# Attention block on one core: the score matmuls of a VectorE row are released together and picked by free heads, and the order is laid out anew

## The chip, the core and the metric

One core of a Trainium2 chip runs the whole kernel. The metric is the time of one launch in device microseconds; lower is better. The engines named here are TensorE (PE; its weight loads are PEld), ScalarE (ACT), VectorE (DVE), GpSimd (POOL) and the DMA queue of SyncE (SP).

## The reference

Self-attention over 2048 tokens, 16 heads of 28, all data in bf16:

```python
B, S, D = x.shape            # 1, 2048, 448
qkv = (x @ wqkv).reshape(B, S, 3, 16, 28).transpose(2, 0, 3, 1, 4)
scores = einsum("bhqd,bhkd->bhqk", q, k) * 28 ** -0.5
p = softmax(scores, axis=-1)
o = einsum("bhqk,bhkd->bhqd", p, v)
return o.transpose(0, 2, 1, 3).reshape(B, S, D) @ wo
```

## The kernel before

**Tiling.** The heads form 4 groups of 4, the queries 4 chunks of 512. A pair of group and chunk is a *unit* (16 of them, 0 to 15). A unit has 16 *rows*, one for each 128 keys, and a row has 4 *tiles*, one a head: 128 keys by 512 queries. That makes 256 rows and 1024 tiles. The head h of a group lies on the partitions 32h to 32h+27 of QT and KT, so a tile's score matmul uses one quarter of TensorE's rows, and matmuls of different heads can stand in the array together.

**Two ways for exp.** 189 rows take the exponential on ScalarE: their 756 tiles are taken in turn in groups of three and two; one *score group* S0, S1, ... is one matmul a tile into three banks of PSUM (0 to 2) or two (3 and 4), and one activation E0, E1, ... (L950) turns the group into PT. So even groups are three-wide, odd ones two-wide, 303 in all, and group i+2 needs the banks that E*i* has read. The other 67 rows (PLAN["rows"]) go to VectorE: each of their tiles has a score matmul of its own (SD*row*_*head*, here a *ride*) into one bank of the pool M (banks 5 to 7), VectorE turns it into integers whose bits are an exponential (D1, L912, into DY), and when the row has all four, two more passes over the row (DS, L920) make shifted copies.

**Behind the scores.** A PV pass is four matmuls, one a head, side by side in TensorE's columns: one pass for a ScalarE row (PT with V), three for a VectorE row (DY with V, DS with VW), all added up in one bank of M for a unit. When a unit is done, VectorE copies the bank to OTS, and the row sums are inverted and spread over the partitions: by DMAs through DRAM for most units, by small fp32 matmuls for unit 14 (N1, L748, and N2, L759) and unit 15. After the last group's units come the output projections (OP, L700). The projections of x to q, k and v (L545, four passes a job; L562, four steps a job) also go through the banks of M, spread over the first 11 units by the due times in PLAN["late"].

**What sets the order.** Every operation is an entry with an engine, its dependencies, a guessed duration and a priority. schedule() plays the engines forward in time: on each it takes, of the entries that could start within a look-ahead of the earliest one (CFG["plook"], 477 ns, on TensorE), the one of least priority. A ride's priority carries CFG["sdpen"] if the entry before it on TensorE is no score matmul. The guessed durations come from pe_dur(): a step within a kind 220 ns, a switch between score matmuls (kind "r") and passes (kind "c") 100 more, a score matmul behind one without a common head 60. Where TensorE would do too little in a window, fill_to() puts in zero passes (L474) or pads a score group with zero matmuls (L891). Each engine then runs its list strictly in that order and waits by semaphores, so the guesses set the order, not the time.

The score group and its activation:

```python
s = P.add("pe", (lambda e, ...: s_mm(e, tl, range(bf(), bf() + 3), DH, s_op[0].pad)), deps=deps, after=[last_s[0]],
          kind="r", units=1.0, act=112.0 * len(tl), heads=tuple(h for _, _, h in tl), ..., name=f"S{gi}", ...)
ex = P.add("act", (lambda e, ...: e.activation(PT[:, p0 * 512:(p0 + w) * 512], bank(bf(), w), AF.Exp, scale=ESCALE)),
           deps=[s] + ..., after=[last_exp[0]], dur=66 + w * 426.67, prio=pr, name=f"E{gi}", ...)
```

A ride (in row_tile): it may not stand ahead of its partner, the group that it was released with.

```python
s = P.add("pe", (lambda e, ...: s_mm(e, [t], [hold[0].banks[0]], DH)), deps=deps, after=[partner, old],
          kind="r", units=1.0, act=112.0, heads=(h,), prio=p_pr + 0.0001, name=f"SD{r}_{h}", acq=("M", 1), acq_slack=ASLACK)
s.ride = True
```

Of the kernel before, what the change touches and what calls it, by code (L numbers as in the profile page):

```python
# [63 lines left out]
class _Prog:  # L64
# [49 lines left out]
    def pe_dur(self, prev, op, t):  # L114

        if op.kind is None:
            return op.dur
        one, switch = (430.0 if t < self.COLD else 220.0), 100.0
        if prev is None or prev.kind != op.kind:
            return switch + one * op.units  # L120
        if op.kind == "r" and op.heads and not set(op.heads) & set(prev.heads):
            return 60.0
        return one * op.units

    def schedule(self):
        ops = self.ops
# [16 lines left out]
        order = {e: [] for e in ENGINES}  # L143
        nsched = 0
        pools = self.pools
        acc_open = [None]
        recent = []

        def fill_to(st, nxt):

# [39 lines left out]
        while nsched < n:  # L190
            best = None
            for e in ENGINES:
                if not avail[e]:
                    continue
                ft = free_t[e]
                sts = [(start_of(i, ft), i) for i in avail[e]]
                sts = [(a, i) for a, i in sts if a is not None]
                if not sts:
                    continue
                mn = min(a for a, i in sts)  # L200
                look = CFG["dlook"] if e == "dve" else CFG["plook"] if e == "pe" else self.BIGLOOK
                cand = [(a, i) for a, i in sts if a <= mn + look]
                off = CFG["sdpen"] if e == "pe" and not (order[e] and order[e][-1].kind == "r") else 0.0
                st, i = min(cand, key=lambda t: (ops[t[1]].prio + (off if ops[t[1]].ride else 0.0), t[1]))
                if st > mn + min(self.LOOKAHEAD, look):
                    fit = [(a, k) for a, k in sts if a <= mn + min(self.LOOKAHEAD, look) and a + ops[k].dur <= st]
                    if fit:
                        st, i = min(fit, key=lambda t: (ops[t[1]].prio, t[1]))
                if best is None or (st, ops[i].prio, i) < best[0]:
                    best = ((st, ops[i].prio, i), e, i)  # L210
# [125 lines left out]
ZLO = -ZADD  # L336


CFG = {"late": 4.5, "load": 1.5, "load0": 18, "dcost": 2.3, "dlead": 31.565328345, "aslack": 232.311784294, "opp": 0.0, "oload": 2.5, "klead": 0.388752986, "vlag": 0.115386484, "hot1": 45000.0, "hotm": 3600.0, "nslack": 2278.659670856, "dlook": 20.0, "plook": 477.119826734, "rcost": 4.9, "rlead": 1.0, "rend": 4, "rgap": 2, "acost": 0.4455, "dprio": 0.137295812, "nride": 2, "rslack": 300.0, "stail": 24, "jprio": -2.367501222, "vwlead": 0.517534586, "sdpen": 6.828329237, "rcostx": -0.000676632}

PLAN = {
    "rows": [9, 14, 19, 21, 26, 32, 36, 37, 43, 48, 51, 54, 57, 58, 61, 67, 74, 78, 83, 85, 90, 95, 96, 99, 103, 104, 107, 111, 113, 118, 119, 126, 128, 133, 136, 142, 143, 145, 147, 155, 160, 164, 170, 171, 175, 176, 180, 181, 187, 190, 192, 194, 197, 199, 207, 208, 211, 215, 216, 219, 221, 228, 229, 232, 239, 242, 243],
    "late": [1.299322759, 1.822557006, 2.163875537, 1.596356936, 2.063296816, 1.856206612, 1.946155059, 2.196917245, 2.351631723, 2.650591028, 2.763613996, 3.528403009, 3.047534614, 3.721148513, 4.223385591, 3.69651624, 3.88002907, 4.051839957, 4.449835317, 4.560752685, 5.643247141, 5.99397256, 6.330386924, 6.513825751, 5.809406098, 6.003720398, 6.187280726, 6.225029866, 8.237463635, 8.012219161, 7.61108487, 7.334748232, 7.574370741, 6.838411391, 7.65064537, 7.734259839, 8.315962664, 7.954788714],
}


def _fast(nc, x, wqkv, wo, out, n_heads=16):
# [35 lines left out]
    with es:  # L383
# [543 lines left out]
        for gi, (kind, idx, b0) in enumerate(items):  # L927
# [14 lines left out]
            else:  # L942
# [5 lines left out]
            s_op.append(s)  # L948
            last_s[0] = s
            ex = P.add("act", (lambda e, p0=p0, w=w, bf=bf: e.activation(PT[:, p0 * 512:(p0 + w) * 512], bank(bf(), w), AF.Exp, scale=ESCALE)),  # L950
                       deps=[s] + [slot_last.get(("A", p0 + j)) for j in range(w)], after=[last_exp[0]], dur=66 + w * 426.67, prio=pr, name=f"E{gi}",
                       rel=[(s, 0)] if b0 is None else [])
            last_exp[0] = ex
            ex.relpool = [("T", b) for b, k_ in t_free.items() if k_ == gi]
# [779 lines left out]
```

## Time and profile before

| | before |
|---|---|
| median of 3 runs | 363.78 us (363.62 to 364.08) |
| the profiled execution | 364.01 us, span 362.2 us |
| granted TensorE clock | 1.00 |
| PE busy | 350.9 us (97%), 3894 matmuls |
| ACT busy | 345.9 us (95%), 303 of 307 instructions are exps |
| DVE busy | 321.4 us (89%), 574 instructions |
| HBM read, written | 7.23 MB, 2.06 MB |

Busy times are of the span. TensorE's matmuls are pipelined and their ends are modelled; ScalarE's recorded durations overlap, an exp's record beginning before that of the last one ends. What an exp or a matmul costs is therefore read from the start of one to the start of the next.

### The profile page before, as it was taken

To read this page: it belongs to the slowest core of one execution; us is meant where nothing else is said; L and a number is where in the kernel's file an instruction comes from. 1 tells how busy PE (TensorE), PEld (TensorE's weight loads), DVE (VectorE), ACT (ScalarE), POOL (GpSimd) and SP (SyncE) were. 2 spreads that over 40 slices of the span, in tenths; PEclk is the share of its full clock that TensorE was granted. 3 is DMA by queue.
4 is the path that set the end of the run, shared out by engine and by line. 5 is a ranking of instruction groups with operands and counts; after the bars stand their busy time and mean duration, and the time that the engine had idled before them with its cause. 6 is when DMAs were issued, how large, how long until landed. Compare 5 with 4: busy or idle time off the path is not lost.

```text
span 362.2 us, 8855 instructions
## 1 busy us (share of the span) xinstructions
PE 350.9 (97%) x3894; PEld 118.1 (33%) x3894; DVE 321.4 (89%) x574; ACT 345.9 (95%) x307; POOL 3.4 (1%) x9
## 2 busy tenths in 40 slices
PE   8999999999999999999999999999999999999996
PEld 4443233233333323232233343322222222223423
DVE  6678978888998899999999999899999999999624
ACT  1999999999999999999999999999999999999892
POOL 3000000000000000000000000000000000000000
PEclk9999999999999999999999999999999999999999
DMA  8500000000000000010000100000000000010111
GB/s 238 144 2 3 4 30 3 21 14 4 30 2 5 32 5 31 2 32 2 3 32 6 33 3 31 2 5 30 4 31 11 23 4 32 2 62 22 53 53 53
DMA packets 12549, 9.93 MB, mean 27 GB/s; under 512 B 4768, under 2 KB 10656, under 8 KB 12504
## 3 DMA queue, kind: packets, MB, share of 16 engines
q1 hardware_dynamic: 11704, 8.63, 8.1%
q8 instruction: 32, 0.52, 0.6%
q10 hardware_dynamic: 800, 0.66, 0.5%
q14 instruction: 13, 0.11, 0.1%
HBM read 7.23 MB, written 2.06 MB: 26 GB/s over the span
## 4 chain that ended last, share of the span: by engine, by line
ACT 73%; PE 23%; DVE 3%; issue 0%
ACT PT L950 73%; PE ps L888 8%; PE ps L855 7%; PE ps L474 2%; PE ps L700 2%; PE ps L545 2%; DVE DY L912 2%; PE ps L562 1%; PE ps L528 1%; PE ps L779 1%; DVE DS L920 0%; PE ps L759 0%; PE ps L822 0%; PE ps L798 0%; PE ps L748 0%
## 5 line engine op out<-in xcount | busy, mean ns | idle before, releaser
L950 ACT ACTIVATE PT<-ps 128x1536 bf16<-128x1536 f32 (+1 forms) x303 | 342.9, 1356 | 1.9 <-PE ps L888 1.1
L912 DVE TENSOR_SCALAR DY<-ps 128x512 int16<-128x512 f32 x268 | 174.6, 682 | 10.7 <-PE ps L888 10.0
L888 PE MATMUL ps<-QT,KT 28*128 28x512 bf16 x1024 | 164.1, 383 | 6.2 <-ACT PT L950 2.7
L920 DVE TENSOR_SCALAR DS<-DY 128x2048 int16<-128x2048 int16 x134 | 90.0, 680 | 0.6
L888 PEld LDWEIGHTS ps<-QT,KT 28*128 28x128 bf16 x1024 | 42.2, 91 | 127.4 <-ACT PT L950 84.4
L855 PE MATMUL ps<-PT,V 128*32 128x512 bf16 x756 | 66.0, 386 | 0.5 <-DVE OTS L713 0.2
L855 PE MATMUL ps<-DS,VW 128*32 128x512 f16 x536 | 47.4, 384 | 0.2 <-DVE DS L920 0.2
L545 PE MATMUL ps<-xT,w_raw 112*32 112x512 bf16 x512 | 36.1, 382 | 0.0
L474 PE MATMUL ps<-ZM,ZW 128*32 128x512 bf16 x316 | 28.6, 410 | 1.2 <-DVE ZM L456 1.2
L855 PEld LDWEIGHTS ps<-PT,V 128*32 128x32 bf16 x756 | 16.7, 94 | 34.7 <-issue 28.7
L855 PE MATMUL ps<-DY,V 128*32 128x512 f16 x268 | 26.4, 385 | 0.2
L855 PEld LDWEIGHTS ps<-DS,VW 128*32 128x32 bf16 x536 | 12.7, 94 | 18.3 <-issue 12.8
L545 PEld LDWEIGHTS ps<-xT,w_raw 112*32 112x32 bf16 x512 | 12.7, 96 | 15.0 <-issue 4.2
L562 PE MATMUL ps<-w_raw,xT 112*128 112x112 bf16 x256 | 17.1, 214 | 0.0
L688 DVE CAST OUTS<-ps 128x448 bf16<-128x448 f32 x14 | 8.7, 620 | 8.2 <-PE ps L700 7.4
L562 PEld LDWEIGHTS ps<-w_raw,xT 112*128 112x128 bf16 x256 | 13.0, 98 | 7.1 <-issue 4.2
L518 DVE CAST KT<-ps 128x512 bf16<-128x512 f32 x16 | 11.0, 686 | 4.6 <-PE ps L545 4.6
L474 PEld LDWEIGHTS ps<-ZM,ZW 128*32 128x32 bf16 x316 | 7.7, 99 | 15.2 <-issue 11.4
L518 DVE CAST V<-ps 128x448 bf16<-128x448 f32 x16 | 9.9, 619 | 3.1 <-PE ps L562 3.1
L700 PE MATMUL ps<-wop,XO 128*128 128x448 bf16 x48 | 11.7, 356 | 0.0
L516 DVE TENSOR_SCALAR QT<-ps 128x512 bf16<-128x512 f32 x15 | 10.3, 687 | 1.1 <-PE ps L545 1.1
L855 PEld LDWEIGHTS ps<-DY,V 128*32 128x32 bf16 x268 | 7.0, 94 | 11.4 <-issue 7.7
(51 smaller groups left out, 85.6 us busy)
## 6 DMA issues: line engine op xcount, KB each, us to landing
RB<-scr_r SPq DMA_DIRECT2D x14, 256.0 KB
out_dram<-OUTS SPq DMA_DIRECT2D x14, 112.0 KB, 1.7
XO<-in_x_dram SPq DMA_DIRECT2D x3, 448.0 KB, 8.0
w_raw<-in_wqkv_dram SPq DMA_DIRECT2D x2, 392.0 KB, 7.4
wop<-in_wo_dram SPq DMA_DIRECT2D x16, 24.5 KB
XO<-in_x_dram SPq DMA_DIRECT2D x1, 224.0 KB, 3.7
XO<-in_x_dram ACTq DMA_DIRECT2D x1, 224.0 KB, 4.0
scr_l<-OTS SPq DMA_DIRECT2D x14, 8.0 KB
```

The lines of the kernel that those rows point to most:

```text
L474: ins = e.matmul(ps[32 * h:32 * h + 32, b * 512:(b + 1) * 512], ZW[:, :], ZM[:, :], start=shut, stop=shut, skip_group_check=not shut, tile ...
L516: fe = (lambda e: e.tensor_scalar(evac[0](), evac[1](hold[0].banks[0]), mul, None, ALU.mult))
L518: fe = (lambda e: e.tensor_copy(evac[0](), evac[1](hold[0].banks[0])))
L545: ins = e.matmul(ps[32 * h:32 * h + 32, b * 512:(b + 1) * 512], w_raw[0:IT, it, col:col + 32], xT[0:IT, it, c * 512:(c + 1) * 512], start= ...
L562: ins = e.matmul(ps[:, b * 512 + j * GD:b * 512 + (j + 1) * GD], xT[0:IT, it, n * 128:(n + 1) * 128], w_raw[0:IT, it, 2 * D + g * GD:2 * D ...
L688: fe = (lambda e: e.tensor_copy(OUTS[:, oi, :], bank(hold.banks[0])[:, 0:D]))
L700: return e.matmul(bank(hold[0].banks[0])[:, 0:D], OTN[:, gg, n * 128:(n + 1) * 128], wop[:, gg, :], start=(gg == 0), stop=(gg == G - 1))
L855: ins = e.matmul(ps[32 * h:32 * h + 32, b * 512:(b + 1) * 512], weights(k, h), p_[h], start=(kt == 0 and k == 0), stop=(kt == NK - 1 and k ...
L888: ins = e.matmul(bank(b), KT[32 * h:32 * h + rows, g, kt * 128:(kt + 1) * 128], QT[32 * h:32 * h + rows, g, c * QCH:(c + 1) * QCH], start= ...
L912: o1 = P.add("dve", (lambda e, ri=ri, h=h, s=s: e.tensor_scalar(DY[:, ri, h * 512:(h + 1) * 512], bank(s.banks[0]), ZLO, ZADD, ALU.max, AL ...
L920: row_ev[r] = [P.add("dve", (lambda e, k=k: e.tensor_scalar(DS[:, k, rk, :], DY[:, ri, :], float(PHASE[k + 1]), None, ALU.add)), deps=row_ ...
L950: ex = P.add("act", (lambda e, p0=p0, w=w, bf=bf: e.activation(PT[:, p0 * 512:(p0 + w) * 512], bank(bf(), w), AF.Exp, scale=ESCALE)), deps ...
```

## The change

1. *Release.* Before, a score group released at most two rides, of heads that it doesn't hold itself and that the row still lacked (nride 2). Now the first group that comes near enough to a row (dlead) releases the row's four rides at once.
2. *Choice.* schedule() keeps run_heads, the heads of the score matmuls that stand directly behind each other at the end of TensorE's list; another kind of entry, or a head that comes a second time, empties it. A ride's priority now carries sdpen if the run is empty, sdlap if it shares a head with the run, and nothing if it doesn't. pe_dur() compares with the run too, not with the last entry alone.
3. *Guess.* The planner's duration of an exp is 51 + w * 426.67 ns instead of 66 + w * 426.67.
4. *Layout.* PLAN["rows"] (67 rows as before, others), PLAN["late"] and ten of CFG's other weights have new values.

```diff
-        if op.kind == "r" and op.heads and not set(op.heads) & set(prev.heads):
+        if op.kind == "r" and op.heads and not set(op.heads) & self.run_heads:
             return 60.0
...
+        run_heads = self.run_heads = set()
...
-                off = CFG["sdpen"] if e == "pe" and not (order[e] and order[e][-1].kind == "r") else 0.0
-                st, i = min(cand, key=lambda t: (ops[t[1]].prio + (off if ops[t[1]].ride else 0.0), t[1]))
+                run = run_heads if e == "pe" else None
+                st, i = min(cand, key=lambda t: (ops[t[1]].prio + (0.0 if not ops[t[1]].ride else CFG["sdpen"] if not run else CFG["sdlap"] if set(ops[t[1]].heads) & run else 0.0), t[1]))
...
                 recent.append((op.t1, op.act))
+                if op.kind != "r" or (run_heads & set(op.heads)):
+                    run_heads.clear()
+                if op.kind == "r":
+                    run_heads.update(op.heads)
...
-CFG = {..., "dlead": 31.565328345, ..., "dprio": 0.137295812, "nride": 2, ..., "sdpen": 6.828329237, ...}
+CFG = {..., "dlead": 28.484612267, ..., "dprio": 0.366065749, "nride": 4, ..., "sdlap": 2.562717941, ..., "sdpen": 5.516852626, ...}
 PLAN = {
-    "rows": [9, 14, 19, 21, 26, 32, 36, 37, 43, ...],
+    "rows": [8, 14, 21, 23, 24, 28, 36, 40, 41, ...],
...
-                       ..., dur=66 + w * 426.67, prio=pr, name=f"E{gi}",
+                       ..., dur=51 + w * 426.67, prio=pr, name=f"E{gi}",
...
-                for h in free[:CFG["nride"]]:
+                for h in (free[:int(CFG["nride"])] if CFG["nride"] < 4 else (3, 2, 1, 0)):
                     have.append(h)
                     row_tile(r, h, s, pr - 5)
```

The file grows by five lines ahead of the kernel's body: L888 becomes L893, L545 L550, L562 L567, L855 L860, L700 L705, L748 L753, L759 L764, L474 L479, L912 L917, L920 L925 and L950 L955.

Two places on TensorE. First the window behind a two-wide score group into which a projection's four passes were put, near a third of the run. Before, score group 96 (heads 0, 1, 2), a ride of head 1 (the row that waits for f_dve), group 97 (two-wide), two PV passes, the projection, group 98:

```order
L888 MATMUL ps<-QT,KT 128x512 [waits f_act]
L888 MATMUL ps<-QT,KT 128x512 x2
L888 MATMUL ps<-QT,KT 128x512 [waits f_dve]
L888 MATMUL ps<-QT,KT 128x512 [waits f_act]
L888 MATMUL ps<-QT,KT 128x512
L855 MATMUL ps<-PT,V 32x512 x8
L545 MATMUL ps<-xT,w_raw 32x512 [waits f_dve]
L545 MATMUL ps<-xT,w_raw 32x512 x15
L888 MATMUL ps<-QT,KT 128x512 [waits f_act]
```

Now, at such a place: group 81 (two-wide, heads 3 and 0), a ride of head 2, one PV pass, a projection, group 82:

```order
L893 MATMUL ps<-QT,KT 128x512 [waits f_act]
L893 MATMUL ps<-QT,KT 128x512
L893 MATMUL ps<-QT,KT 128x512 [waits f_dve]
L860 MATMUL ps<-PT,V 32x512 x4
L550 MATMUL ps<-xT,w_raw 32x512 [waits f_dve]
L550 MATMUL ps<-xT,w_raw 32x512 x15
L893 MATMUL ps<-QT,KT 128x512 [waits f_act]
```

The ride has moved from behind a group that shares its head to behind one that doesn't, and one PV pass has left the window.

Second the normalisation of unit 14 in the tail. Before, its second half (L759, three quarters and then the last one behind three zero passes) stands behind group 288, which is three-wide, after an output projection:

```order
L888 MATMUL ps<-QT,KT 128x512 [waits f_act]
L888 MATMUL ps<-QT,KT 128x512 x2
L700 MATMUL ps<-wop,XO 128x448 [waits f_dve]
L700 MATMUL ps<-wop,XO 128x448 x3
L759 MATMUL ps<-id_f,RS 32x128 [waits f_dve]
L759 MATMUL ps<-id_f,RS 32x128 x11
L474 MATMUL ps<-ZM,ZW 32x512 x12
L759 MATMUL ps<-id_f,RS 32x128 x4
```

Now it stands behind group 287, which is two-wide and directly follows group 286:

```order
L893 MATMUL ps<-QT,KT 128x512 [waits f_act]
L893 MATMUL ps<-QT,KT 128x512 x2
L893 MATMUL ps<-QT,KT 128x512 [waits f_act]
L893 MATMUL ps<-QT,KT 128x512
L479 MATMUL ps<-ZM,ZW 32x512 x8
L705 MATMUL ps<-wop,XO 128x448 [waits f_dve]
L705 MATMUL ps<-wop,XO 128x448 x3
L764 MATMUL ps<-id_f,RS 32x128 [waits f_dve]
L764 MATMUL ps<-id_f,RS 32x128 x15
```

The zero passes have moved ahead of the output projection and are two instead of three, and the whole second half stands in one piece, one group earlier.

More of the change, by code (lines that the diff above doesn't have):

```diff
@@ L336 @@
 ZLO = -ZADD
-CFG = {"late": 4.5, "load": 1.5, "load0": 18, "dcost": 2.3, "dlead": 31.565328345, "aslack": 232.311784294, "opp": 0.0, "oload": 2.5, "klead": 0.388752986, "vlag": 0.115386484, "hot1": 45000.0, "hotm": 3600.0, "nslack": 2278.659670856, "dlook": 20.0, "plook": 477.119826734, "rcost": 4.9, "rlead": 1.0, "rend": 4, "rgap": 2, "acost": 0.4455, "dprio": 0.137295812, "nride": 2, "rslack": 300.0, "stail": 24, "jprio": -2.367501222, "vwlead": 0.517534586, "sdpen": 6.828329237, "rcostx": -0.000676632}
+CFG = {"late": 4.5, "load": 1.5, "load0": 18, "dcost": 2.3, "dlead": 28.484612267, "aslack": 234.39592858, "opp": 0.0, "oload": 2.5, "klead": 0.4323975, "vlag": 0.111436825, "hot1": 45000.0, "hotm": 3600.0, "nslack": 2491.286802307, "dlook": 20.0, "plook": 475.978771878, "rcost": 4.9, "rlead": 1.0, "rend": 4, "rgap": 2, "acost": 0.4455, "dprio": 0.366065749, "nride": 4, "rslack": 300.0, "stail": 24, "jprio": -1.39984025, "sdlap": 2.562717941, "vwlead": 0.511450916, "sdpen": 5.516852626, "rcostx": -0.000676632}
@@ L341 @@
 PLAN = {
-    "rows": [9, 14, 19, 21, 26, 32, 36, 37, 43, 48, 51, 54, 57, 58, 61, 67, 74, 78, 83, 85, 90, 95, 96, 99, 103, 104, 107, 111, 113, 118, 119, 126, 128, 133, 136, 142, 143, 145, 147, 155, 160, 164, 170, 171, 175, 176, 180, 181, 187, 190, 192, 194, 197, 199, 207, 208, 211, 215, 216, 219, 221, 228, 229, 232, 239, 242, 243],
-    "late": [1.299322759, 1.822557006, 2.163875537, 1.596356936, 2.063296816, 1.856206612, 1.946155059, 2.196917245, 2.351631723, 2.650591028, 2.763613996, 3.528403009, 3.047534614, 3.721148513, 4.223385591, 3.69651624, 3.88002907, 4.051839957, 4.449835317, 4.560752685, 5.643247141, 5.99397256, 6.330386924, 6.513825751, 5.809406098, 6.003720398, 6.187280726, 6.225029866, 8.237463635, 8.012219161, 7.61108487, 7.334748232, 7.574370741, 6.838411391, 7.65064537, 7.734259839, 8.315962664, 7.954788714],
+    "rows": [8, 14, 21, 23, 24, 28, 36, 40, 41, 49, 50, 52, 53, 56, 63, 69, 70, 75, 81, 84, 92, 95, 96, 99, 103, 107, 109, 111, 114, 118, 120, 126, 133, 134, 135, 140, 141, 145, 150, 151, 161, 164, 165, 172, 174, 176, 177, 181, 184, 187, 190, 191, 193, 198, 200, 209, 210, 212, 218, 220, 222, 229, 232, 234, 236, 242, 243],
@@ new lines @@
+    "late": [0.985671578, 1.7329246, 2.288014113, 1.339252415, 3.3302101, 1.724823683, 1.811463685, 2.191018136, 2.31384295, 2.705035917, 3.075950617, 3.785215586, 3.262105589, 3.600600612, 4.037198031, 4.358459457, 3.422715306, 4.857595707, 4.052828262, 4.565812919, 5.085450579, 6.945699915, 6.701297875, 7.57212228, 5.328799148, 5.744658604, 6.006846096, 6.663843099, 7.985857407, 10.303312002, 7.510487333, 7.372796781, 7.921217652, 7.444661772, 7.671904113, 8.161370786, 7.99358382, 8.734219075],
@@ L950, in _fast @@
             ex = P.add("act", (lambda e, p0=p0, w=w, bf=bf: e.activation(PT[:, p0 * 512:(p0 + w) * 512], bank(bf(), w), AF.Exp, scale=ESCALE)),
-                       deps=[s] + [slot_last.get(("A", p0 + j)) for j in range(w)], after=[last_exp[0]], dur=66 + w * 426.67, prio=pr, name=f"E{gi}",
+                       deps=[s] + [slot_last.get(("A", p0 + j)) for j in range(w)], after=[last_exp[0]], dur=51 + w * 426.67, prio=pr, name=f"E{gi}",
                        rel=[(s, 0)] if b0 is None else [])
```

## The prediction

> **What bounds the kernel now.** I read the page first: busy times, the chain that ended last, the costliest groups.
>
> ```profile
> PE 350.9 (97%) x3894; PEld 118.1 (33%) x3894; DVE 321.4 (89%) x574; ACT 345.9 (95%) x307; POOL 3.4 (1%) x9
> ACT 73%; PE 23%; DVE 3%; issue 0%
> L950 ACT ACTIVATE PT<-ps 128x1536 bf16<-128x1536 f32 (+1 forms) x303 | 342.9, 1356 | 1.9 <-PE ps L888 1.1
> ```
>
> ScalarE is busy nearly from end to end with 303 exps (L950). By the group's row only 1.9 us of idle time stand before them, which would leave a new order nothing to win. But recorded exps overlap, so that idle time hides lateness, and I read the starts instead, from the timeline of ScalarE (start, duration; each row is from a window so narrow that it holds few exps): the first exp, two undisturbed ones, three pairs of which the second is late, and the last exp.
>
> ```profile
> 10.28 1.45 ACT L950 ACTIVATE PT<-ps 128x1536 bf16<-128x1536 f32 x1 [0.71 <-PE ps L891]
> ...
> 46.35 1.53 ACT L950 ACTIVATE PT<-ps 128x1536 bf16<-128x1536 f32 x1
> 47.68 1.12 ACT L950 ACTIVATE PT<-ps 128x1024 bf16<-128x1024 f32 x1
> ...
> 67.81 1.34 ACT L950 ACTIVATE PT<-ps 128x1024 bf16<-128x1024 f32 x1
> ...
> 99.70 1.08 ACT L950 ACTIVATE PT<-ps 128x1024 bf16<-128x1024 f32 x1
> 100.96 1.45 ACT L950 ACTIVATE PT<-ps 128x1536 bf16<-128x1536 f32 x1 [0.18 <-PE ps L888]
> ...
> 120.36 1.12 ACT L950 ACTIVATE PT<-ps 128x1024 bf16<-128x1024 f32 x1
> 121.44 1.45 ACT L950 ACTIVATE PT<-ps 128x1536 bf16<-128x1536 f32 x1
> ...
> 222.72 1.09 ACT L950 ACTIVATE PT<-ps 128x1024 bf16<-128x1024 f32 x1
> 223.81 1.45 ACT L950 ACTIVATE PT<-ps 128x1536 bf16<-128x1536 f32 x1
> ...
> 353.69 0.74 ACT L950 ACTIVATE PT<-ps 128x512 bf16<-128x512 f32 x1
> ```
>
> A three-wide exp holds ScalarE for 47.68 - 46.35 = 1.33 us. Between 47.68 and 67.81 lie nine undisturbed pairs: 20.13 / 9 = 2.237 us a pair, so a two-wide one takes 0.90. The 151 pairs from 10.28 to 353.69 would need 337.7 us and take 343.4: **5.7 us are lost** to late starts. The exp at 100.96 is late by 1.26 - 0.90 = 0.36 us, though its row names 0.18. That loss is what the change can touch; everything else is 151 pairs, a start and a tail.
>
> Why exps start late shows on TensorE. Here it works up to the exp at 121.44 (PEld row: weight load of score group 97; PE rows: its matmuls are not a row of their own, the merged row before them is left out):
>
> ```profile
> 119.27 0.09 PEld L888 LDWEIGHTS ps<-QT,KT 28*128 28x128 bf16 x2 [0.60 <-ACT PT L950]
> ...
> 119.59 0.61 PE L855 MATMUL ps<-PT,V 128*32 128x512 bf16 x8
> 120.03 1.04 PE L545 MATMUL ps<-xT,w_raw 112*32 112x512 bf16 x16
> 121.00 0.39 PE L888 MATMUL ps<-QT,KT 28*128 28x512 bf16 x4
> 121.33 0.40 PE L855 MATMUL ps<-PT,V 128*32 128x512 bf16 x4
> 121.55 0.39 PE L855 MATMUL ps<-DY,V 128*32 128x512 f16 x4
> 121.87 0.39 PE L888 MATMUL ps<-QT,KT 28*128 28x512 bf16 x3
> 122.19 0.62 PE L855 MATMUL ps<-DS,VW 128*32 128x512 f16 x8
> 122.74 0.60 PE L888 MATMUL ps<-QT,KT 28*128 28x512 bf16 x4
> ```
>
> The two-wide group 97 gets its banks at 119.27, which is 0.24 after the exp before its own began (120.36 - 1.33). Then come two PV passes, four projection passes and, at 121.00, the three-wide group 98; its exp begins 0.44 later and 0.18 late. So between a two-wide group and the next three-wide one TensorE has 1.33 + 0.90 - 0.44 - 0.24 = **1.55 us**; this window took 1.73. Between a three-wide group and a two-wide one there is some 0.4 us more to spare, and overruns can be carried.
>
> Step prices from the same rows: pass to pass 0.22 (121.33 to 121.55); pass to scores 0.32 (121.55 to 121.87); scores to pass 0.32 (121.87 to 122.19). A VectorE score tile (a "ride") next to a group that leaves its head free adds nothing: group 98 with its ride has x4 in 0.39, as three matmuls have. With a common head it adds a pass: x4 in 0.60 at 122.74.
>
> **The change: work on TensorE.** I counted both orders step by step. Neighbouring score tiles with a common head: 160 before, 64 now; of the rides directly behind a group, 88 shared a head and now 2 do. That is 96 x 0.21 = 20.2 us less. But score work is entered and left more often, 304 times against 284: 20 x (0.32 + 0.32 - 0.22) = 8.4 us more. Net TensorE needs about 11.8 us less.
>
> The Trainium skill ("TensorE: Matmul & The Clock Gate", Back-to-back issue gap) gives 131 ns for a 512-column matmul in a sustained stream; by that the 96 conflicts would be worth only 12.6 us and the net 4.2. The row of 0.60 against 0.39 disagrees with it here, and I go by the row.
>
> The Trainium skill ("TensorEngine Tiling (Array Packing)", Key Properties) also speaks against the new order: changing the tiling mode drains the array, a price that the 20 new visits pay. The trace agrees (0.32 instead of 0.22 a switch), and the 8.4 us hold it.
>
> TensorE's saved time is no saved time of the kernel: most of it only lengthens waits for ScalarE. It counts where a window ran over. So I split the 5.7 us.
>
> (1) Over-full windows. By these prices ten two-wide windows before the tail need over 1.55 us (behind groups 79, 81, 87, 97, 163, 165, 173, 175, 179, 187: mostly five or six passes), together 2.1 us over. Eight of the exps behind them are late, by 1.67 us together, from 100.96 (0.36) through 121.44 (0.18) to 223.81 (1.09 - 0.90 = 0.19). In the new order there are five (137, 157, 195, 197, 267), together 0.83 over; in the same proportion 0.66 late. Gain 1.0. Windows such as the one behind the new group 81 (ride, PV, four projections: 0.01 + 0.31 + 4 x 0.216 + 0.32 = 1.50) now fit.
>
> (2) Four late exps behind full windows in a row (128, 130, 192, 274), 0.5 us; the same tally gives two now (104, 136), 0.35. Gain 0.15.
>
> (3) The remaining late starts before the tail: 5.7 - 1.3 (the tail, below) - 1.67 - 0.5 = 2.2 us, some 18 of 0.03 to 0.17 us and many smaller. Their windows fit by the prices, and most hold a ride, so I put them to rides that wait for VectorE to empty a bank, and to steps a little over price. A row of the waits (us, times, longest), two of the groups and one of the windows (stretch, length, busy us and counts by engine, granted clock, DMA):
>
> ```profile
> PEld ps L888 <- DVE DY L912: 20.3, 60, 0.5
> L891 PE MATMUL ps<-ZM 28*128 28x512 bf16 x17 | 2.3, 374 | 0.0
> L474 PE MATMUL ps<-ZM,ZW 128*32 128x512 bf16 x316 | 28.6, 410 | 1.2 <-DVE ZM L456 1.2
> 60.00:330.00 270.00, 264.45 (x2938) 83.12 (x2935) 258.95 (x454) 269.73 (x240) 0.00 (x0) 1.00 0.06 17
> ```
>
> Rides wait for VectorE 60 times, 0.34 us each. The bounds of this term: all 2.2 us stay, or they shrink like the rest of the tally (2.5 us of overrun before the tail becomes 1.1, carried lateness included), a gain of 1.2. More slack behind a ride helps, the wait itself stays: I take 0.5, nearer to the first. In it are the padding matmuls (L891), 3 instead of 17, inside score groups.
>
> (4) The tail, where unit 14's normalisation stands between score groups (ScalarE, then TensorE):
>
> ```profile
> 334.45 1.58 ACT L950 ACTIVATE PT<-ps 128x1536 bf16<-128x1536 f32 x1
> 336.26 2.37 ACT L950 ACTIVATE PT<-ps 128x1024 bf16<-128x1024 f32 x2 [0.23 <-PE ps L888]
> 337.18 1.44 ACT L950 ACTIVATE PT<-ps 128x1536 bf16<-128x1536 f32 x1
> 339.36 1.02 ACT L950 ACTIVATE PT<-ps 128x1024 bf16<-128x1024 f32 x1 [0.74 <-PE ps L888]
> ...
> 334.18 0.93 PE L700 MATMUL ps<-wop,XO 128*128 128x448 bf16 x4
> 334.95 0.95 PE L748 MATMUL ps<-SEL,OTS 128*128 128x4 f32 x8
> ...
> 336.41 0.93 PE L700 MATMUL ps<-wop,XO 128*128 128x448 bf16 x4
> 337.27 0.86 PE L759 MATMUL ps<-id_f,RS 128*32 128x128 f32 x24
> 337.95 0.83 PE L474 MATMUL ps<-ZM,ZW 128*32 128x512 bf16 x12
> 338.60 0.40 PE L759 MATMUL ps<-id_f,RS 128*32 128x128 f32 x8
> ```
>
> Exps 287 and 289 are late by 1.81 - 1.33 = 0.48 and 2.18 - 1.33 = 0.85, 1.33 us together. The change takes one output projection from behind group 286 and a zero pass (337.95, three before, two now), but puts each half of the normalisation behind a two-wide group, where there is less room. Added up from these rows, the new windows behind 285, 287 and 289 run over by 0.4, 0.9 and 0.4; the same addition gives 1.9 for before where 1.33 was measured, so 1.2 is left. Gain 0.15, between -0.4 and 0.5.
>
> Free or equal: exp, VectorE and DMA instructions are the same in kind and number; TensorE's order is the same up to score group 2 and behind the last group, so start (10.28) and tail after 353.69 stay. The zero passes stay 316 matmuls. The planner's exp price (66 to 51 ns) only orders.
>
> Sum: 1.0 + 0.15 + 0.5 + 0.15 = **1.8 us** less. The profiled execution took 364.01 (span 362.2), so 362.2; the median of the runs is 0.23 lower, 363.78 - 1.8 = **362.0 us**. From the terms' bounds (1.0 within 0.6 to 1.2) this case lies between 360.8 and 363.0. About 0.2%, 0.73 us, is what a measurement of this kernel can tell from no change.
>
> **Rivals.**
>
> *Slower: rides block TensorE's queue.* All four tiles of a row stand ready now, and 149 of them directly behind a group whose head they don't touch (54 before). Each still waits for VectorE to empty one of three banks, with PV passes and the next group behind it. In the new order 40 two-wide windows hold a ride and have under 0.34 us to spare; a wait of 0.34 in each would run over by 6.9 us. VectorE is busy 89% of the span and its 60 waits speak for it; that TensorE already waits for it before, for a share of 2.2 us only, against. It decides from about 2.5 of the 6.9 us; with half of them, 362.0 + 3.4 = 365.4. Chance 0.09. The Trainium skill ("TensorE: Matmul & The Clock Gate", Part 3) says that matmuls start and end strictly in order, which is this mechanism; the chance rests on the rows.
>
> *Slower: the granted clock.* Less work on TensorE could let its clock drop; it was 1.00 throughout 60 to 330 us. A pass would double to 0.43: a stretch of three exps (3.4 us) with some 2.6 us of steps would need 5.2, about 1.8 us late; three such stretches give 367. The unchanged zero passes speak against it. Chance 0.03.
>
> *No change.* The late starts are VectorE's more than TensorE's conflicts, term (3) stays whole, the tail loses its 0.4, and the new over-full windows cost their full 0.83: gain 0.4, 363.4. Chance 0.14.
>
> *Much faster.* Terms (1) to (3) vanish altogether: 363.78 - 4.4 = 359.4. Chance 0.06. That the change doesn't do what it says is out: the order shows 2 conflicts behind groups where 88 stood.
>
> **How the numbers follow.** The forecast has 0.68. Its upper end (363.0 to 363.05) still counts as faster, so faster has 0.68 + 0.06 = 0.74, no change 0.14, slower 0.12. The range: below 360.8 lies most of the much faster case, above 363.7 the slower ones and a little of no change, together under 0.2.
>
> **What would show it.** In the profile after: late starts from first to last exp of about 3.9 us instead of 5.7; rides within 0.39 us of their group; waits of L888's weight loads for ScalarE above 84 us; start and end of the exp stream apart by about 341.6. Wrong: waits for VectorE far above 20.3 us with late exps behind rides; a clock below 1.00; late exps in the tail above 1.8 us.

## The result and the profile after

The changed kernel took 366.5 us (median of 9 runs, 364.85 to 373.66), the kernel before 363.78 (9 runs, 363.62 to 364.16). The ratio is 1.0048 [1.0031, 1.0065]; it leaves out the longest runs, 372 to 374 us, in which TensorE's clock was at half speed for about 20 us. The forecast of 362.0 us was wrong in sign.

The profiled execution was one of those long ones (373.66 us, span 371.5). The same kernel was profiled once more at full clock (after_again below): 365.24 us, span 363.1. Both are needed. First the page of the long one: its span, busy times, ScalarE's slices, the granted clock in tenths over 40 slices, the chain, and the exps' group (busy, mean ns, idle).

```profile
span 371.5 us, 8829 instructions
PE 353.1 (95%) x3880; PEld 115.1 (31%) x3880; DVE 324.8 (87%) x574; ACT 346.8 (93%) x307; POOL 3.4 (1%) x9
ACT  1999999999999999999999766999999999999892
PEclk9999999999999999999999655999999999999999
ACT 73%; PE 21%; DMA 2%; DVE 2%; issue 1%; SPq 0%
L955 ACT ACTIVATE PT<-ps 128x1536 bf16<-128x1536 f32 (+1 forms) x303 | 343.8, 1388 | 10.5 <-PE ps L893 9.4
```

Before, every digit of PEclk was 9 and 1.9 us of idle time stood before the exps:

```profile
PEclk9999999999999999999999999999999999999999
```

Now 10.5 us of idle time do, three slices show a clock of 0.5 to 0.6, and ScalarE starves in the same three. The damage has a place, 204 to 232 us. The timeline there, TensorE with its weight loads, and one row of ScalarE:

```profile
204.91 0.10 PEld L860 LDWEIGHTS ps<-PT,V 128*32 128x32 bf16 x4 [0.23 <-issue]
204.92 0.40 PE L860 MATMUL ps<-PT,V 128*32 128x512 bf16 x4
...
205.34 0.39 PE L893 MATMUL ps<-QT,KT 28*128 28x512 bf16 x2
...
207.20 0.40 PE L860 MATMUL ps<-PT,V 128*32 128x512 bf16 x4 [1.48 <-issue]
...
208.21 0.62 PE L860 MATMUL ps<-DS,VW 128*32 128x512 f16 x4
...
209.41 2.37 ACT L955 ACTIVATE PT<-ps 128x1536 bf16<-128x1536 f32 x2 [1.87 <-PE ps L893]
```

At 205.72 TensorE stops for 1.48 us with "issue" as the reason: it waits for nothing that the profile shows. Behind the stop, passes of 0.40 us become passes of 0.62. The exp at 209.41 (E174) starts 2.13 us late, where before's E174 was 0.20 late. The next view cuts the profile into stretches (length; busy us and counts by engine; granted clock; DMA), with the cuts put where the trace's clock record changes:

```profile
201.03:204.44 3.41, 3.41 (x52) 1.64 (x50) 2.69 (x7) 3.41 (x4) 0.00 (x0) 1.00 0.07 26
204.45:207.86 3.41, 1.91 (x23) 0.51 (x19) 2.44 (x5) 3.09 (x3) 0.00 (x0) 1.00 0.02 5
207.87:231.75 23.88, 23.88 (x159) 4.44 (x158) 15.86 (x26) 16.00 (x14) 0.00 (x0) 0.50 0.03 9
231.76:235.17 3.41, 3.41 (x37) 0.93 (x33) 2.99 (x6) 3.41 (x4) 0.00 (x0) 1.00 0.07 26
```

A stretch of 3.41 us holding the stop (TensorE busy for 1.91 of it) is followed by 23.88 us at exactly half clock, seven times 3.41. In the profile at full clock the same stop, 1.20 us, falls otherwise into the stretches, and the clock stays:

```profile
206.86 0.40 PE L860 MATMUL ps<-PT,V 128*32 128x512 bf16 x4 [1.20 <-issue]
...
203.56:206.97 3.41, 2.19 (x34) 0.73 (x30) 3.26 (x7) 3.41 (x4) 0.00 (x0) 1.00 0.02 5
206.98:210.39 3.41, 3.16 (x36) 0.85 (x28) 2.55 (x5) 2.39 (x3) 0.00 (x0) 1.00 0.02 5
```

Late starts from E0 to E302, counted as the prediction does but with 50.6 + 426.67 ns a tile as an exp's price (1.331 us three-wide, 0.904 two-wide; the rows gave 1.33 and 0.90): 6.00 us before, 15.39 in the long profile, 7.03 in the one at full clock.

**What stops TensorE.** The trace records a taken branch of TensorE there, from 205.33 to 207.14. The program holds a second, general path for inputs that the fast one does not cover, and it lies in the middle of each engine's code. The fast path jumps over it at a named operation; a hint at another named operation announces the jump (PV8_8 is the PV pass of unit 8 and row 8; a third number, as in PV8_8_1, counts the passes of a VectorE row from the second one on):

```python
P.HINT_AT = {"pe": "PV8_8", "dve": f"NM{NU - 2}", "act": exps[-6]}
P.JUMP_AT = {"pe": "PV8_11", "dve": f"OPEV{n0 - 1}", "act": f"OPEV{n0}", "sp": "L1_0"}
```

The diff does not touch these lines, but it moves what stands between the two names. From hint to jump it was 5.12 us before (196.28 to 201.40); in the new order it is 3.17 us (202.16 to 205.33). One 16 KB packet on queue 8 follows the hint; by its time it brings the target's code. The DMA view of 204.7 to 205.9 us in the long profile holds just that packet (packets, MB, share):

```profile
q8 instruction: 1, 0.02, 5.0%
```

It ran from 204.80 to 205.76, when TensorE had been at the jump since 205.33; the jump ended 1.39 us after the landing. Before, it ran from 197.83 to 198.81, long ahead of the jump, which took 0.33 us. The Trainium skill ("Runtime: NRT & Kernel Launch", Instruction fetch mechanics) says that instructions are prefetched in sequence only, in blocks of 16 KiB, and that a taken branch to a page that isn't there waits for its DMA. The stop agrees; in the kernel before, where a packet came behind the hint and ahead of the jump, the jump had nothing to wait for.

### The profile page after: what moved, and what is told of

Read it like the earlier page. It is cut to its first block, busy times and chain, and to the rows that moved or that the text cites. A ratio compares the mean times of both kernels' runs of the same rounds, so it can differ in the third digit from the quotient of the medians.

```text
span 371.5 us, 8829 instructions
## 1 busy us (share of the span) xinstructions
PE 353.1 (95%) x3880; PEld 115.1 (31%) x3880; DVE 324.8 (87%) x574; ACT 346.8 (93%) x307; POOL 3.4 (1%) x9
## 4 chain that ended last, share of the span: by engine, by line
ACT 73%; PE 21%; DMA 2%; DVE 2%; issue 1%; SPq 0%
ACT PT L955 73%; PE ps L893 8%; PE ps L860 7%; PE ps L550 2%; DMA XO<-in_x_dram 2%; PE ps L479 1%; PE ps L567 1%; PE ps L705 1%; PE ps L784 1%; DVE DY L917 1%; DVE DS L925 0%; PE ps L753 0%; PE ps L764 0%; PE ps L827 0%; PE ps L803 0%
## 5 line engine op out<-in xcount | busy, mean ns | idle before, releaser
L955 ACT ACTIVATE PT<-ps 128x1536 bf16<-128x1536 f32 (+1 forms) x303 | 343.8, 1388 | 10.5 <-PE ps L893 9.4
L917 DVE TENSOR_SCALAR DY<-ps 128x512 int16<-128x512 f32 x268 | 176.7, 686 | 17.1 <-PE ps L893 16.0
L893 PE MATMUL ps<-QT,KT 28*128 28x512 bf16 x1024 | 156.3, 395 | 11.4 <-ACT PT L955 6.7
L925 DVE TENSOR_SCALAR DS<-DY 128x2048 int16<-128x2048 int16 x134 | 90.0, 684 | 0.7
L893 PEld LDWEIGHTS ps<-QT,KT 28*128 28x128 bf16 x1024 | 39.5, 91 | 140.6 <-ACT PT L955 96.1
L860 PE MATMUL ps<-PT,V 128*32 128x512 bf16 x756 | 68.2, 394 | 2.4 <-issue 1.5
L860 PE MATMUL ps<-DS,VW 128*32 128x512 f16 x536 | 50.3, 398 | 0.0
L550 PE MATMUL ps<-xT,w_raw 112*32 112x512 bf16 x512 | 36.8, 389 | 0.2
L479 PE MATMUL ps<-ZM,ZW 128*32 128x512 bf16 x316 | 29.8, 425 | 1.2 <-DVE ZM L461 1.2
L860 PEld LDWEIGHTS ps<-PT,V 128*32 128x32 bf16 x756 | 17.2, 94 | 33.3 <-issue 25.4
L860 PE MATMUL ps<-DY,V 128*32 128x512 f16 x268 | 27.1, 395 | 0.2 <-DVE OTS L718 0.2
L860 PEld LDWEIGHTS ps<-DS,VW 128*32 128x32 bf16 x536 | 12.3, 94 | 22.4 <-issue 15.7
L567 PE MATMUL ps<-w_raw,xT 112*128 112x112 bf16 x256 | 17.3, 214 | 0.0
L550 PEld LDWEIGHTS ps<-xT,w_raw 112*32 112x32 bf16 x512 | 12.6, 97 | 13.7 <-issue 3.8
L567 PEld LDWEIGHTS ps<-w_raw,xT 112*128 112x128 bf16 x256 | 13.0, 98 | 6.5 <-issue 4.3
L479 PEld LDWEIGHTS ps<-ZM,ZW 128*32 128x32 bf16 x316 | 7.6, 99 | 14.1 <-issue 11.6
L705 PE MATMUL ps<-wop,XO 128*128 128x448 bf16 x48 | 11.5, 355 | 0.0
L718 DVE COPY OTS<-ps 128x512 f32<-128x512 f32 x15 | 10.3, 686 | 0.6 <-PE ps L860 0.6
```

What stands on the lines that cost most here:

```text
L479: ins = e.matmul(ps[32 * h:32 * h + 32, b * 512:(b + 1) * 512], ZW[:, :], ZM[:, :], start=shut, stop=shut, skip_group_check=not shut, tile ...
L550: ins = e.matmul(ps[32 * h:32 * h + 32, b * 512:(b + 1) * 512], w_raw[0:IT, it, col:col + 32], xT[0:IT, it, c * 512:(c + 1) * 512], start= ...
L567: ins = e.matmul(ps[:, b * 512 + j * GD:b * 512 + (j + 1) * GD], xT[0:IT, it, n * 128:(n + 1) * 128], w_raw[0:IT, it, 2 * D + g * GD:2 * D ...
L705: return e.matmul(bank(hold[0].banks[0])[:, 0:D], OTN[:, gg, n * 128:(n + 1) * 128], wop[:, gg, :], start=(gg == 0), stop=(gg == G - 1))
L718: accev = P.add("dve", (lambda e: e.tensor_copy(OTS[:, ub, :], bank(pv_open[u].banks[0]))), deps=[last_pv, ots_last[ub]], dur=610, prio=pr ...
L860: ins = e.matmul(ps[32 * h:32 * h + 32, b * 512:(b + 1) * 512], weights(k, h), p_[h], start=(kt == 0 and k == 0), stop=(kt == NK - 1 and k ...
```

## The experiments

### The hint earlier and later

Theory: the stop is what made the change slower. Rival: the new order's rides and windows did. Four kernels on one chip.

```diff
 # after_hint_early (the changed kernel)       | after_again: the changed kernel as it is
-P.HINT_AT = {"pe": "PV8_8", ...
+P.HINT_AT = {"pe": "PV8_6", ...
 # before_hint_late (the kernel before)
+P.HINT_AT = {"pe": "PV8_8_1", ...
 # before_hint_early (the kernel before)
+P.HINT_AT = {"pe": "PV8_3", ...
```

> The new order with one edit: TensorE's branch hint stands about 9 us ahead of its jump instead of 3.2 us. Theory A (the jump's target is not loaded in time, and the stop lets the clock drop): the jump takes 0.4 us or less instead of 1.8, exp 174 is late by under 0.3 instead of 2.1, the clock stays 1.00 in every run, and the time is 362.5 to 363.3. Theory B (rides or thin stretches of the new order make it slower by themselves): the time stays at 364.8 or more, or the clock still drops in some runs.

> The kernel before with its hint about 3.4 us ahead of the jump instead of 5.1. Theory A: the jump takes 1.4 to 1.8 us instead of 0.33, the exp behind it is 1.2 to 2 us late, time 364.8 to 365.8, and some runs with a lower clock. Theory B: no change from 363.8, since the old order does not suffer.

> The new order unchanged, on the same chip. Both theories: 364.8 to 367 with the clock at 1.00 or 0.995, and up to 373 where the clock drops for some 24 us; the jump at about 205 us takes 1.8 us in every run.

> The kernel before with its hint about 9.7 us ahead of the jump instead of 5.1: a control. Theory A: the jump takes 0.1 to 0.33 us, and the time is 363.5 to 363.8. If the hint's place cost something by itself, the time would rise.

Measured, against 363.8 us before: after_hint_early 364.27 (12 runs, ratio 1.0013 [0.9992, 1.0033]), after_again 365.78 (12 runs, 1.0057 [1.0026, 1.0088]), before_hint_early 363.74 (0.9997 [0.9977, 1.0016]), before_hint_late 363.83 (1.0003 [0.9977, 1.0029]). In after_hint_early the jump takes 0.335 us, E174 is 0.08 late, and the timeline at the jump shows no stop (but the time misses theory A's 362.5 to 363.3, and two of its 12 runs show a clock of 0.995):

```profile
205.22 0.39 PE L893 MATMUL ps<-QT,KT 28*128 28x512 bf16 x2
...
205.61 0.40 PE L860 MATMUL ps<-PT,V 128*32 128x512 bf16 x4
205.84 0.39 PE L860 MATMUL ps<-DY,V 128*32 128x512 f16 x4
```

So the stop carries most of the loss, and what is left of the new order is no gain. before_hint_late missed: its hint stood 3.69 us ahead of the jump, the packet landed at 199.69, 1.56 us before the jump began, and that was in time (0.44 us).

### The stop alone, in the old order

```diff
 # before_hint_2us (the kernel before)
-P.HINT_AT = {"pe": "PV8_8", ...
+P.HINT_AT = {"pe": "SD143_3", ...
 # before_hint_at_jump (the kernel before)
+P.HINT_AT = {"pe": "PV8_11", ...
```

> The order before, untouched, but the hint that announces TensorE's jump stands at SD143_3, about 2.2 us ahead of the jump at PV8_11 instead of 5.1. Theory of the stop (the changed kernel lost its time because its new order left only 3.2 us between hint and jump): the instruction page starts to load about 1.3 us behind the hint, takes 1.0 us, and the jump ends about 1.4 us after it has landed, so the jump takes 1.2 to 1.6 us instead of 0.33; the exp behind it starts 1 to 1.5 us late instead of 0.2 to 0.3, the time is 364.8 to 365.3 against 363.8, and some of the executions show a granted clock of 0.995 or less, up to 8 us longer, as those of the changed kernel do. Rival (the new order itself draws the lower clock, by its mode changes and zero passes): the jump may take 1.2 to 1.6 us, but no execution of this one falls below a clock of 0.999 more often than the kernel before does (1 of 35).

> The order before, untouched, with the hint directly ahead of the jump at PV8_11. By the rule found (page load starts 1.15 to 1.55 us behind the hint, takes about 1.0 us, the jump ends 1.38 us behind the landing) the jump takes 3.5 to 3.9 us. Theory (the half clock is granted by what TensorE did in a fixed stretch of 3.413 us: of two stops in the changed kernel the one that left a stretch busy for 0.56 was followed by half clock and the one that left 0.64 was not): a stop of 3.6 us leaves some stretch busy for under 0.53 however it falls, so nearly every run, 10 of 12 or more, shows a clock of 0.995 or less, also in the old order; the time is 367 to 368 by the stop alone and up to 376 with seven stretches at half clock. Rival (the new order draws the lower clock, not the stop): at most 2 of 12 below 0.998, the time 366.8 to 367.3 throughout.

before_hint_2us took 364.56 us (11 runs, ratio 1.0035 [1.0011, 1.0060]), 0.2 below the expected range: the stop was 0.80 us, and of the expected 1 to 1.5 us of lateness only E170's 0.74 arrived. Two of 11 runs had a clock of 0.99 or less, too few against the kernel before (4 of some 95 runs of these experiments) to tell theory from rival. before_hint_at_jump tells them apart: 371.05 us (5 runs, 370.38 to 371.15, 1.0189 [1.0175, 1.0203]), every one at a clock of 0.985 or 0.986. Its timeline (one row each of TensorE and ScalarE) and its stretches:

```profile
204.80 0.40 PE L855 MATMUL ps<-PT,V 128*32 128x512 bf16 x4 [3.22 <-issue]
...
205.79 1.45 ACT L950 ACTIVATE PT<-ps 128x1536 bf16<-128x1536 f32 x1 [3.00 <-PE ps L888]
...
202.27:205.67 3.40, 0.87 (x11) 0.22 (x11) 0.58 (x1) 0.52 (x1) 0.00 (x0) 1.00 0.07 23
205.68:215.91 10.23, 10.23 (x80) 2.21 (x77) 5.85 (x9) 6.89 (x6) 0.00 (x0) 0.50 0.01 2
215.92:219.33 3.41, 3.41 (x39) 1.42 (x35) 3.16 (x6) 2.62 (x3) 0.00 (x0) 1.00 0.01 2
```

A one-word edit to the untouched old order makes it 7.2 us slower: a stop of 3.2 us, then three times 3.41 us at half clock, in which E171 to E176 start 4.6 us late together. The stop, and not the new order, lowers the clock here. The jumps side by side (us; from the trace's records of the hint, the next 16 KB packet behind it and the branch; the last two kernels come further below):

| kernel | hint to jump | packet starts, after the hint | landed, against the jump's start | jump took | from landing to its end |
|---|---|---|---|---|---|
| before | 5.12 | 1.55 | 2.60 ahead | 0.33 | |
| before_hint_late | 3.69 | 1.12 | 1.56 ahead | 0.44 | |
| before_hint_2us | 2.48 | 1.14 | 0.16 ahead | 1.22 | 1.38 |
| before_hint_at_jump | 0.11 | 1.06 | 2.20 behind | 3.53 | 1.33 |
| after | 3.17 | 2.64 | 0.43 behind | 1.81 | 1.39 |
| after_again | 3.17 | 2.34 | 0.16 behind | 1.54 | 1.38 |
| before_hint_early | 9.66 | 1.35 | 7.38 ahead | 0.34 | |
| after_hint_early | 9.04 | 4.66 | 3.39 ahead | 0.34 | |
| rule_old_layout | 6.61 | 1.58 | 3.90 ahead | 0.34 | |
| layout_old_rule | 6.15 | 1.96 | 3.19 ahead | 0.34 | |

In the changed kernel the packet starts later behind its hint than in the first four. There another page had been loading from 200.86 to 202.13, until just before the hint (after_again: 201.00 to 202.42, past it); in the first four the last load ended 2 us or more ahead of the hint. layout_old_rule fits: a load ended 0.26 us ahead of its hint, and its packet starts 1.96 behind it. So the new order was hit twice: less distance, and, by these three traces, a hint close behind a page load. The early hints look different. after_hint_early has a single packet from 190 us to the jump, at 200.84, where the changed kernel loads the other page, and 31 packets on queue 8 in all instead of 32 (before_hint_early has 31 too). What that packet holds the trace does not say; the page was there at the jump.

### The early hint once more

> The changed kernel with the early hint once more, on the same chip as the one above. Theory (with the stop gone the new order keeps a lower clock in some runs, fewer than the 10 of 22 of the changed kernel): 2 to 5 of 12 runs below 0.998, those at 364.9 to 366, the others at 363.9 to 364.5, median 364.2 to 364.5. Rival (only the stop lowers the clock): none below 0.998.

364.11 us (11 runs, 1.0014 [0.9995, 1.0033]), one run at a clock of 0.991, between the theory's two to five and the rival's none: this run alone decides for neither. Together, 3 of 23 runs are below 0.998 with the hint early and 10 of 22 without it.

### The rule and the layout apart

```diff
 # rule_old_layout: the changed code with the numbers of before    # layout_old_rule: the old code with the new numbers
-CFG = {..., "nride": 4, ...}  PLAN (new)  dur=51 + w * 426.67     -CFG = {..., "nride": 2, ...}  PLAN (old)  dur=66 + w * 426.67
+CFG = {..., "nride": 2, ...}  PLAN (old)  dur=66 + w * 426.67     +CFG = {..., "nride": 2, ...}  PLAN (new)  dur=51 + w * 426.67
```

nride is 2 in both, and the hint is at PV8_6. With nride 2 the changed code still releases at most two rides a group, heads that the group doesn't hold. So, other than the first text says, rule_old_layout has the new choice but the old release, and no run has the release by itself. What the texts call mode changes are neighbouring score tiles with a common head.

> The change's code (the four score matmuls of a VectorE row released together, the next one chosen by the heads that the running group leaves free) with the numbers of before (rows, due times, costs), hint early. Theory (the numbers were fitted to the old rule, so the rule alone breaks their fit): mode changes fall from 160 to about 90, but more windows hold more passes than their exp lasts, the late starts grow from 6.0 to 9 to 11 us and the time is 366.5 to 369. Rival (mode changes are what the rule is worth, 70 fewer by 0.1 to 0.2 us in windows that are full): faster than 363.8 by 0.5 to 1.5 us.

> The new numbers (rows, due times, costs) with the old rule: the score matmuls of a row released one at a time, chosen without a look at the heads; hint early. Theory: numbers and rule fit only together; mode changes stay high (about 140), the late starts grow to 12 to 17 us, the time is 370 to 375. Rival (the layout is good by itself and the rule adds little): within 1 us of 363.8.

rule_old_layout took 369.41 us (1.015 [1.0135, 1.0165]), layout_old_rule 377.84 (1.0381 [1.0366, 1.0396]): the theory's sign, 0.4 and 2.8 above its ranges. The jump takes 0.34 us in both, so no stop is in these times; the late starts are 12.7 and 17.6 us. TensorE's rows of layout_old_rule around exp 240 show one place where a mismatch costs:

```profile
290.50 0.38 PE L888 MATMUL ps<-QT,KT 28*128 28x512 bf16 x1
290.81 0.40 PE L474 MATMUL ps<-ZM,ZW 128*32 128x512 bf16 x4
291.14 0.39 PE L888 MATMUL ps<-QT,KT 28*128 28x512 bf16 x1
291.46 0.40 PE L474 MATMUL ps<-ZM,ZW 128*32 128x512 bf16 x4
291.79 0.38 PE L888 MATMUL ps<-QT,KT 28*128 28x512 bf16 x1
292.11 0.83 PE L474 MATMUL ps<-ZM,ZW 128*32 128x512 bf16 x12
```

Single rides follow each other at 0.64 us with zero passes between them, near the rate at which VectorE empties banks (three D1 in 1.88 us at 291.17; DVE is busy for all of the 10 us from 284 to 294), and the next score group stands behind them: E240 starts 3.9 us late. That is what the prediction's rival of rides that block the queue looks like. It shows here, where rule and layout don't belong together, and not in the changed kernel; how much of the 17.6 us it makes was not counted.

### The remaining late starts by hand

```diff
 # after_mended: the early hint, and behind P.schedule()
+for nm, behind in (("PV3_5_2", "SD63_2"), ("PV6_12", "SD114_3"), ("PV9_9", "SD165_0"), ("PV13_14_2", "SD234_1"), ...):
+    move(at(nm), behind)          # 12 PV passes and 1 ride, out of over-full two-wide windows
+...                               # tail: OP4 behind S286, the zero passes and PV15_1 behind S288, OP6 and OP7 one group later
 # after_mended_fill: and nine zero passes emitted twice
+for n in (76, 63, 61, 60, 59, 53, 51, 41, 28):
+    pe.insert(zs[n - 1], pe[zs[n - 1]])
```

> The changed kernel with three edits: the hint at PV8_6 (9.0 us ahead of the jump), thirteen PV passes and rides moved by hand out of score windows that hold more TensorE work than their exp lasts into the next window of three tiles, and the last windows laid out so that E286 and E288 find their scores ready. Theory (with the hint early the new order loses 1.01 us to E138, E158, E196 and E268, 0.44 to E104 and E136, some 0.5 to E70, E78, E82, E194 and E252, and 1.53 to E286 and E288, each because too many passes stand ahead of its score): these starts come on time, E286 and E288 lose 0.5 together, and the time falls from 364.3 to 362.2 to 363.2, below the kernel before at 363.8. Rival (these exps wait for the matmuls' sources, not for the passes ahead of them, or the moved passes make the next exps late by as much): 363.9 to 364.4, the late time in other places.

> The changed kernel with the early hint and the mended order, and nine zero passes (36 matmuls) doubled in place where TensorE stands idle for 0.19 to 0.31 us ahead of score groups (around 158, 214, 255, 274 to 279 and 312 us). Theory (the runs at clock 0.995, which cost 1.2 to 1.7 us, come from stretches in which the new order, with 96 mode changes fewer, leaves TensorE too little to do; in the mended order's profile 276.5 to 279.9 us is busy for 0.80 only): those runs become rare, at most 2 of 12, and the median falls to 363.2 to 363.6, below the kernel before at 363.8. Rival (those stretches are not what lets the clock fall): as many runs at 0.995 as without, 5 of 12 or so, median 364 to 365. Of the 0.35 us that the new order takes behind its last instruction neither theory says anything; the run shows whether 36 more matmuls move it.

> The mended order unchanged, beside the one with nine zero passes more, on the same chip. Theory: runs at clock 0.995 again in 4 to 7 of 12, runs at clock 1.0 at 363.2 to 363.6; a profile of a run at 0.995, if it falls to one, shows a single stretch of 3.4 us at half clock behind 254 to 280 us. Rival: the runs at 0.995 were that chip's or that hour's, and at most 1 of 12 shows it here.

| | runs | median us | ratio | runs below a clock of 0.998 | median of the others |
|---|---|---|---|---|---|
| after_mended | 12 | 364.40 | 1.0009 [0.9997, 1.0021] | 7 | 363.39 |
| after_mended_again | 12 | 363.39 | 0.9997 [0.9973, 1.0022] | 4 | 363.25 |
| after_mended_fill | 12 | 363.55 | 0.9996 [0.9966, 1.0026] | 3 | 363.46 |

The forecast of 362.2 to 363.2 us was missed. In the profile of after_mended the stream loses 5.30 us instead of 5.91. Part of it helped: E136 and E70 are on time, E158, E268 and the tail improve (the tail from 1.53 us in two exps to 0.91 in three), while E102, E104, E138 and E196 stay as late as they were and E82 and E140 become 0.20 and 0.14 later. So "too many passes ahead" is borne out for some of these starts and not shown for the others. At full clock it is 0.4 to 0.5 us faster than the kernel before. Over all runs no interval is clear of 1, because 11 of 24 runs lose 0.8 us or more to a lower clock, without any stop at the jump. Nine zero passes more left 3 of 12, where at most 2 were expected: a smaller share than 11 of 24, but too few runs to call the cause shown. No profile fell on such a run, so where it loses its clock stays open.

## Why the prediction was wrong, point by point

**The steps that failed.** First, the prediction took every late start from the steps within a window, and "everything else is 151 pairs, a start and a tail". A hint and a jump that are bound to two names in TensorE's order were not among the things moved, so the stop at the jump was put at nothing. At full clock the changed kernel takes 365.0 us (12 of 22 runs), 1.2 more than before; with the early hint, at full clock, 364.2. The stop is worth 0.9 us of the 1.2 (365.03 against 364.17). The rest of the median's 2.7 us goes with half clock: 10 of 22 runs, the median one among them, took 366.5 to 373.7. Second, the terms themselves: (1) to (4) were to gain 1.8 us and gained 0.1. That would have made the forecast wrong without any stop. From the forecast of 362.0 to 365.0 at full clock, 1.7 us are the terms, 0.9 the stop, and 0.34 lie outside the span ("Start and tail stay", below).

**Rival "the granted clock".** It was right in kind and had a chance of 0.03. It looked for the idle time in "less work on TensorE" and counted three stretches of 3.4 us; here seven followed the stop in the profile, and by their clocks of 0.995 to 0.971 the other runs had one to six or so.

**TensorE's net 11.8 us.** The page row of after_hint_early and the waits of the score matmuls' weight loads for ScalarE and VectorE (us, times, longest):

```profile
PE 344.4 (95%) x3880; PEld 115.2 (32%) x3880; DVE 323.8 (89%) x574; ACT 345.7 (96%) x307; POOL 3.4 (1%) x9
PEld ps L893 <- ACT PT L955: 101.2, 270, 0.7
PEld ps L893 <- DVE DY L917: 16.7, 47, 0.5
```

Before, the wait for ScalarE was:

```profile
PEld ps L888 <- ACT PT L950: 84.4, 237, 0.9
```

TensorE is busy for 6.5 us less than 350.9, so the direction holds and 11.8 was too much. The waits moved as forecast: for ScalarE from 84.4 to 101.2 us, for VectorE from 20.3 to 16.7. It bought the kernel almost nothing: over the exp stream 6.00 us of late starts became 5.91. By terms, in after_hint_early:

- *(1) Over-full windows, gain 1.0.* Four of the five exps named are late, E138, E158, E196 and E268, with 1.01 us against 0.66 forecast and 1.67 before. Gain 0.66, just inside the bounds of 0.6 to 1.2. Scaling by the old proportion (1.67 late for 2.1 over) was too kind: it is 1.01 late for 0.83 over. Why was not shown.
- *(2) Full windows in a row, gain 0.15.* E104 and E136, as named: 0.44 us after 0.51. Gain 0.07.
- *(3) The other late starts, gain 0.5 (0 to 1.2).* Those over 25 ns add up to 1.70 us, where before had 1.67: the lower bound. Waits for VectorE fell by 3.6 us and this sum did not move, so it does not hang on the total of those waits; what makes each start late was not shown. The lateness below 25 ns rose from 0.82 to 1.22 us, a loss that no term held: 60 of 151 three-wide exps are followed after 1.34 to 1.36 us instead of 39. Its cause was not found.
- *(4) The tail, gain 0.15 (-0.4 to 0.5).* It lost 0.2: E286 and E288 are late by 0.83 and 0.70 us (E287 starts at 336.14), where E287 and E289 were by 0.48 and 0.85. ScalarE's starts, and what TensorE does ahead of group 286's exp:

```profile
331.73 2.56 ACT L955 ACTIVATE PT<-ps 128x1536 bf16<-128x1536 f32 x2
333.06 1.23 ACT L955 ACTIVATE PT<-ps 128x1024 bf16<-128x1024 f32 x1
334.80 1.45 ACT L955 ACTIVATE PT<-ps 128x1536 bf16<-128x1536 f32 x1 [0.50 <-PE ps L893]
...
337.75 1.45 ACT L955 ACTIVATE PT<-ps 128x1536 bf16<-128x1536 f32 x1 [0.59 <-PE ps L893]
...
332.40 0.61 PE L860 MATMUL ps<-PT,V 128*32 128x512 bf16 x8
332.95 0.83 PE L753 MATMUL ps<-SEL,OTS 128*128 128x4 f32 x6
333.71 0.40 PE L479 MATMUL ps<-ZM,ZW 128*32 128x512 bf16 x4
334.04 0.39 PE L753 MATMUL ps<-SEL,OTS 128*128 128x4 f32 x2
334.36 0.60 PE L893 MATMUL ps<-QT,KT 28*128 28x512 bf16 x5
```

  The normalisation's first half now stands in a two-wide window, with two PV passes and a zero pass (332.40 to 334.36), as the prediction said. Its windows ran over by 0.4 (behind 285), 0.9 (287) and 0.4 (289); measured are 0.83, 0.70 and nothing, 1.53 of 1.7, so the discount to 1.2 was wrong; the sum came nearly right, the single windows did not.

**"Start and tail stay".** The exp stream's start and its tail inside the span do (10.28 and 8.53 us; 10.07 and 8.54 with the early hint; E0 itself moves by some 0.3 between profiles of one order). But the time is longer than the span, by 1.78 to 1.87 us in the profiles of the old order and by 2.13 to 2.23 in those of the new one, some 0.34 more, nearly all that the early hint leaves. layout_old_rule has 1.77, rule_old_layout 2.02. Whether this lies ahead of the first recorded instruction or behind the last one the traces don't show, and the cause is open.

**Rivals.** *Rides block the queue*: not here, as the waits show. *No change*, 363.4: nearest to the truth once the hint is early (364.1 to 364.3, 1.0013 and 1.0014 with both intervals including 1).

## What to carry to other kernels

When an edit moves instructions, list everything in the program that is bound to a place in the order, prefetch hints and jumps among them, and measure the distances before and after. An idle gap on TensorE has two prices: its own length, and the half clock that may follow it, which was worth 4.6 us behind a stop of 3.2 and some 8 behind one of 1.5. A scheduling rule and the numbers that were fitted with it are one thing: the new choice with the old numbers cost 5.6 us, the new numbers with the old rule 14.

## What the runs showed of the hardware

- *A jump to a page that isn't loaded.* The packet started 1.06 to 1.55 us behind the hint in four profiles of the old order, where the last page load had ended 2 us or more ahead of it, and 1.96 to 2.64 behind it in three profiles where one ran at the hint or had ended at most 0.26 ahead. It took 0.96 to 1.25 us, and a jump that had to wait ended 1.33 to 1.39 us after the landing. A hint 3.69 us ahead was enough, one 3.17 us ahead behind a page load was not.
- *The half clock comes in stretches of 3.41 us on a grid of its own.* A stretch of 3.41 us in which TensorE was busy for 1.91 was followed by seven stretches at half clock, one with 0.87 by three, one with 2.19 by none; what sets their number is open. In the long profile half clock begins and ends 59 and 66 times 3.413 us behind the first record of full clock, at 6.48 us; in the other profiles that first record lies between 4.0 and 7.1 us. The Trainium skill ("TensorE: Matmul & The Clock Gate", Part 1) gives 3413 ns for a window that runs freely; the rows agree. The same page's rule that there be no idle gaps over about 3.4 us is too weak here: a gap of 1.48 us was enough, though one of 1.20 was not. Busy time alone doesn't decide it either: in rule_old_layout a stretch with 2.9 us busy, mostly single score matmuls, zero matmuls and waits, was followed by one at half clock.
